# Softmax sums of batch 5 on GpSimd, and its key sums four gate slots later, in a fused attention and SwiGLU kernel

## The chip, the cores and the metric

The kernel runs on one core of one Trainium2 chip. The metric is the device time of one execution in microseconds (us), as a median of several runs. The profile shows one further execution; its span (231.4 us) runs from the first to the last instruction.

## The reference, cut to what matters

```python
# q, k, v: (8, 8, 576, 64); phi: (8, 8, 576, 32); batches, heads, positions, width
a = np.exp(phi - phi.max(2)); a = a / (a.sum(2) + 1e-9)
k_m = np.einsum('bhsm,bhsd->bhmd', a, k)      # 576 keys become 32
v_m = np.einsum('bhsm,bhsd->bhmd', a, v)
scores = q @ k_m.T / sqrt(64)
attn_out = softmax(scores) @ v_m
x = attn_out as (8 * 576, 512)
out = (silu(x @ w_gate) * (x @ w_val)) @ w_out     # 512 -> 1536 -> 512
```

What the change touches is the denominator of the first softmax, `np.sum(a, axis=2)`: for each of 8 heads and 32 memory slots, a sum of 576 exponentials. The kernel holds these exponentials of a batch as nine slices of 128 x 128 (`t_ephi`), with 64 of the positions of a head on the partitions, so the denominator is a sum over the nine slices and then over partitions.

## The kernel before, in words

The kernel works through eight batches. Each batch after the first two has a stage with two parts: a dense part, in which TensorE (PE) multiplies the hidden block of the batch before with the output weights and ScalarE and VectorE make the attention of this batch, and then 24 gate slots. A slot is one pair of gate matmuls, a SiLU on ScalarE (`gv_gate`), and the pair of value matmuls of the slot before with its multiplication on VectorE. Matmuls with `t_U` at line 515 are these gate and value products; those at line 727 are the output products (`p_os`, `p_oa`, `p_oc`).

The schedule is written out by hand: each engine runs its instructions in the order in which the program emits them. In the gate part, `spread` merges several streams into one order. A stream is a list of items with a first and a last slot number; item i of n gets the key first + (i + 0.5) * (last - first) / n, and the items are emitted in the order of their keys. The 24 slots have the keys 0.5, 1.5 and so on to 23.5.

Between the slots of batch b lies the preparation of batch b + 1. `kv_items` gives two items: the key and value sums with what goes with them (`run_sums`), and the transposition of the result by a DMA (`kv_T`, from `t_bkv` to `t_kT`). Their stream runs from `KV` = 6 to 10, so they have the keys 7.0 and 9.0: between slots 6 and 7, and between 8 and 9. Beside the sums stands a U round (`u_item(b, 2)`), which the slots from 16 on use, and two output units. At the keys 19 to 20 lies `u_three(b + 1)`, the first user of the transposed keys.

There are two forms of the sums:

- Without help: nine denominator products on TensorE (line 258, one for each slice of `t_ephi`) into a bank of their own, the reciprocal on VectorE, then 72 key and value products (line 230), scaling on VectorE, then the U round and the two units.
- With `phi_sum` (lines 212 to 219): GpSimd (POOL) adds the nine slices in float32 and writes the sum as two bf16 parts, `t_ehl`. Then `run_sums` does the 72 products first, the U round and the two units, and only then two denominator products from `t_ehl`, the reciprocal and the scaling.

Batches 4, 6 and 7 take the second form (`phi_sum(b + 1)` in the stages of batches 3, 5 and 6); batches 2, 3 and 5 take the first.

In the stage of batch 4, GpSimd has a further job. Each batch has 576 positions, of which 64 are left over by the tiling of the output products; those of four batches are collected and multiplied together. `quad_sums(0)` makes the sums for that, twelve additions and subtractions on GpSimd (`t_Q` and `t_x`, lines 664 and 560). It starts behind `wait_for(atts[4, 1])`, a small copy that holds GpSimd's queue until the normalized scores of batch 4 exist (`t_mark<-t_A`). In the gate part the quad's output units lie in slots 0 to 3 (twelve units) and from 12 to 18.5 (thirty units); the last units of batch 3 lie in slots 4 to 7. Between slots 7 and 12 there are gate slots alone. Later in the same stage GpSimd makes the sums of the hidden blocks of batch 4 (`t_S`, from line 603 on), and issues the loads of batch 7.

Of the kernel before, what the change touches and what calls it, by code (L numbers as in the profile page):

```python
# [14 lines left out]
def kernel(  # L15
# [59 lines left out]
    def bank(shape, dtype, name):  # L75
        tag = free.pop(0)
        t = ps.tile(shape, dtype, tag=tag, name=name)
        held[id(t)] = tag, t
        return t

    def done(*tiles):

        for t in tiles:
            free.append(held.pop(id(t))[0])
# [29 lines left out]
    def load_qT(b):  # L114

        qTs[b] = att.tile([128, NS, 128], BF16, tag="qT", name="t_qT")
        nc.sync.dma_start_transpose(out=qTs[b], in_=qs[b])
# [87 lines left out]
    def phi_sum(b):  # L205

        e = ephis[b].rearrange("p j i m -> p j (i m)")
        wait_for(atts[b - 1, 1][0:1, 0, 0:1])  # L210
        t = att.tile([128, 4, 128], FP32, tag="es", bufs=1, name="t_es")
        add = lambda o, x, y: nc.gpsimd.tensor_tensor(out=o, in0=x, in1=y, op=ALU.add)
        add(t, e[:, 0:4], e[:, 4:8])
        add(t[:, 0:2], t[:, 0:2], t[:, 2:4])
        add(t[:, 0], t[:, 0], t[:, 1])
        add(t[:, 0], t[:, 0], e[:, 8])
        hl = att.tile([128, 2, 128], BF16, tag="ehl", bufs=1, name="t_ehl")
        nc.gpsimd.tensor_copy(out=hl[:, 0], in_=t[:, 0])
        nc.gpsimd.tensor_tensor(out=hl[:, 1], in0=t[:, 0], in1=hl[:, 0], op=ALU.subtract)
        esums[b] = hl  # L220

    def kv_sum(b, p, parts):


        w0, w1 = parts[0], parts[-1] + 1
        n = (w1 - w0) * D
        for j in range(JK):
            for i in range(NP):
                for g in range(NG):
                    nc.tensor.matmul(  # L230
                        p[g][32 * i:32 * i + 32, 0:n],
                        lhsT=phi_of(b, g, j, i),
                        rhs=kvs[b][64 * g:64 * g + 64, w0:w1, i, j * D:(j + 1) * D],
                        start=(j == 0),
                        stop=(j == JK - 1),
                        tile_position=(64 * g, 32 * i),
                    )

    def kv_denominators(b, p):

        if b in masked:
            for g in range(NG):
                for j in range(JK):
                    nc.tensor.matmul(
                        p[:, g:g + 1],
                        lhsT=masked[b][:, j, g].rearrange("p i m -> p (i m)"),
                        rhs=ones1,
                        start=(j == 0),
                        stop=(j == JK - 1),
                    )  # L250
            return
        if b in esums:
            hl = esums.pop(b)
            terms = [hl[:, t] for t in range(2)]
        else:
            terms = [ephis[b][:, j].rearrange("p i m -> p (i m)") for j in range(JK)]
        for n, x in enumerate(terms):
            nc.tensor.matmul(p, lhsT=x, rhs=ones2, start=(n == 0), stop=(n == len(terms) - 1))

    def kv_reciprocal(b, p):  # L260
        r = att.tile([128, NG], FP32, tag="rS", name="t_rS")
        nc.vector.reciprocal(out=r, in_=p)
        rSs[b] = r
# [28 lines left out]
    def kv_items(b, beside=None):  # L292


        def run_sums():
            o = 2 * D
            behind = b in esums
            own = beside and not behind
            if own:
                d = bank([128, NG], FP32, "p_S")  # L300
                kv_denominators(b, d)
                kv_reciprocal(b, d)
                done(d)
            p = [bank([128, CH], FP32, f"p_kv{g}") for g in range(NG)]
            if not (own or behind):
                kv_denominators(b, p[0][:, o:o + NG])
            kv_sum(b, p, (0, 1))
            if behind:
                beside()
                kv_denominators(b, p[0][:, o:o + NG])  # L310
            if not own:
                kv_reciprocal(b, p[0][:, o:o + NG])
            kv_norm(b, p)
            if beside and not behind:
                beside()

        return [run_sums, lambda: kv_T(b)]
# [324 lines left out]
    def wait_for(x):  # L642

        t = att.tile([1, 1], BF16, tag="mark", bufs=1, name="t_mark")
        nc.gpsimd.tensor_copy(out=t, in_=x)
# [183 lines left out]
    def q_items(b, evac):  # L829
        return [lambda n=n: q_T(b, n, evac[n]) for n in range(3)]  # L830

    def u_item(b, c, evac="avav"):

        return lambda: u_round(b, (((0,), c, (0, 1)), ((1,), c, (0, 1))), evac)
# [13 lines left out]
    def run(items):  # L848
        for x in items:
            x()  # L850
# [10 lines left out]
    def exp_tables():  # L861
        nc.scalar.preload_act_table_set("natural_log_exp_and_others")
# [111 lines left out]
    def take(n):  # L974
        nonlocal backlog
        n = max(0, min(n, len(backlog)))
        part, backlog = backlog[:n], backlog[n:]
        return part

    KV = 6  # L980
# [15 lines left out]
    for b in range(2, B):  # L996
        last = b + 1 == B
        exp_tables()
        if b == 2:
            load_qT(3)  # L1000
            phi_exp(2)
            (zero, ops0), (one, ops1) = products(0, ("c11",)), products(1, ("p1", "c11"))
            kv, q2 = kv_items(2), q_items(2, "aaa")
            run(zero[:6])
            sums = {n: f for n, f in zip(((1, 1), (0, 2), (1, 2)), late)}
            late.clear()
            sums[0, 2]()
            weight_sums(0)
            weight_sums(1)
            run(zero[6:12] + one[:6] + kv[:1] + q2[:2])  # L1010
            weight_sums(2, (0, 1))
            run(zero[12:16] + zero[18:22] + kv[1:] + q2[2:] + zero[16:18] + zero[22:24])
            weight_sums(2, (2, 3))
            ops0["c11"]()
            ops1["p1"]()
            wait_for(Ts[2][0:1, 3, 0, 0:1])
            for part in ((0, 1), (3,), (2,)):
                for c in (1, 2):
                    sums[1, c](part)
            loads(4)  # L1020
            backlog = one[6:12] + zero[36:] + one[12:36]
            ops = ops1
        else:
            run(take(6))
        for g in range(NG):
            scores(b, g)
        if b > 2:
            ops["p1"]()
            u_values(b)
        else:  # L1030
            run(zero[24:36] + take(6))
        run(take(6))
        z_inv_v(b, 0)
        ops["c11"]()
        run(take(6))
        if not last:
            phi_exp(b + 1)
        z_inv_v(b, 1)
        if b > 2:
            norm(b, 0)  # L1040
            norm(b, 1)
        run(take(6))
        run_late()
        if b == 4:
            wait_for(atts[4, 1][0:1, 0, 0:1])
            quad_sums(0)
        nc.scalar.preload_act_table_set("silu_and_others")
        run(take(6))
        if b == 2:
            norm(2, 0)  # L1050
        run(take(6))
        if b == 2:
            norm(2, 1)
            u_three(2)
            run(one[36:])
        g = gv_slots(b)
        quad = []
        if b == 4:
            quad = products(b, (), 0)[0]
        if last:  # L1060
            rest, rest_ops = products(b, (), 1)
            backlog += rest[:12]
        beside = 0 if last else 2 if quad else min(4, len(backlog))
        outs = [lambda: run(take(1)) for _ in range(len(backlog) - beside)]
        streams = [(g, 0, 24), (quad[:12], 0, 3), (quad[12:], 12, 18.5)]
        streams += [(outs, 4, 7 if quad else 24)]
        if b == 2:
            streams += [([lambda: u_values(2)], 2.5, 3)]
        if last:
            streams += [([u_item(b, 2)], 5, 6)]  # L1070
        if not last:
            if b > 2:
                load_qT(b + 1)
            if b > 2 and b != 4:
                phi_sum(b + 1)
            streams += [
                (kv_items(b + 1, lambda: (u_item(b, 2, "aava")(), run(take(2)))), KV, KV + 4),
                ([lambda: (u_three(b + 1), run(take(2)))], 19, 20),
            ]
        spread(*streams)  # L1080
        flush_mul()
        units, ops = products(b, ("p1", "c11"))
        backlog += units
# [34 lines left out]
```

## Time and profile before

| | |
|---|---|
| time, median of three runs | 233.22 us (233.15 to 233.31) |
| span of the profiled run | 231.4 us |
| mean granted TensorE clock | 0.997 |
| gate part of batch 4 | 123.69 to 143.63 us |
| GpSimd's leftover sums in it | 123.33 to about 130.9 us |
| key sums of batch 5 | from 128.84 us |

In the profile's rows the first number is the start in us from the span's start, the second the duration; then engine, line, operation, output and inputs with their shape, and how many like instructions were merged. [...] the spacing of starts, and not the sum of durations, tells what TensorE's queue pays. A bracket at the end gives the idle time of the engine ahead of the row and what ended it. `PEld` is TensorE's weight load, `DVE` is VectorE, `ACT` ScalarE, `POOL` GpSimd and `SPq` the queue from which stores and transposing DMAs are issued.

### The profile page before, as it was taken

The page shows a single profiled execution, that of the slowest core. Times are in us where ns is not written, and L with a number is a line of the kernel's source. Part 1 is how long each engine was busy: PE and PEld are TensorE (multiplying, and loading weights), DVE is VectorE, ACT ScalarE, POOL GpSimd, SP SyncE. Part 2 cuts the span into 40 slices and gives each one's busy share as a digit, 9 for nine tenths or more (in the row PEclk, how much of TensorE's full clock was granted, in tenths as well). Part 3 has the DMA queues.
Part 4 walks back from the last instruction along what each step waited for, and adds up shares of the span by engine and source line. Part 5 has one row for each costly group of instructions (what it writes and reads, how often), then busy time and mean ns, then how long its engine had stood idle before and what let it go on. Part 6 is the DMA issues. An engine that isn't in the chain of part 4 may idle for free.

```text
span 231.4 us, 7210 instructions
## 1 busy us (share of the span) xinstructions
PE 221.6 (96%) x2825; PEld 169.8 (73%) x2825; DVE 185.1 (80%) x423; ACT 171.7 (74%) x365; POOL 140.8 (61%) x190
## 2 busy tenths in 40 slices
PE   6987799999999999999999999999999999999993
PEld 2544476778887777878788787887788778878882
DVE  4245789999966799989997668998999899977732
ACT  2777898988447989968896658978898789677310
POOL 8422427998199049765977689464845394039291
PEclk9999999999999999999999999999999999999998
DMA  6999999999996992999299946994014502202125
GB/s 214 210 211 206 199 207 207 221 245 268 205 225 175 256 256 49 223 204 184 71 223 191 226 134 115 252 236 89 28 65 114 104 0 95 91 10 84 31 85 160
DMA packets 36674, 36.84 MB, mean 159 GB/s; under 512 B 14624, under 2 KB 31008, under 8 KB 36640
## 3 DMA queue, kind: packets, MB, share of 16 engines
q0 software_dynamic: 16272, 22.42, 52.5%
q1 hardware_dynamic: 19600, 13.18, 22.9%
q10 hardware_dynamic: 768, 0.79, 1.1%
q8 instruction: 22, 0.36, 0.6%
q14 instruction: 12, 0.10, 0.1%
HBM read 42.47 MB, written 9.44 MB: 224 GB/s over the span
## 4 chain that ended last, share of the span: by engine, by line
PE 86%; DMA 9%; POOL 2%; ACT 1%; issue 0%; DVE 0%; POOLq 0%
PE p_g L515 21%; PE p_os L727 21%; PE p_v L515 20%; PE p_oc L727 10%; DMA W<-in_moe_w_val_dram 9%; PE p_oa L727 5%; PE p_u L472 5%; PE p_kv L230 2%; PE p_g L396 1%; POOL t_kv L99 1%; POOL t_kv L103 1%; PE p_q L383 0%; POOL t_q L108 0%; ACT t_qT L337 0%; POOL W L138 0%
## 5 line engine op out<-in xcount | busy, mean ns | idle before, releaser
L538 DVE TENSOR_TENSOR t_h<-t_sg,p_v 128x288 bf16<-128x288 bf16 x192 | 81.8, 451 | 14.1 <-PE p_v L515 7.0
L515 PEld LDWEIGHTS <-t_U 128*128 128x128 bf16 x768 | 73.9, 98 | 21.2 <-issue 3.5
L532 ACT ACTIVATE t_sg<-p_g 128x288 bf16<-128x288 f32 x192 | 73.3, 424 | 17.1 <-PE p_g L515 11.4
L515 PE MATMUL p_g<-t_A,t_U 128*128 128x288 bf16 x384 | 77.0, 286 | 0.0
L515 PE MATMUL p_v<-t_A,t_U 128*128 128x288 bf16 x384 | 77.0, 286 | 0.0
L727 PEld LDWEIGHTS <-t_S 128*128 128x128 bf16 x384 | 37.5, 98 | 4.5 <-issue 0.2
L603 POOL TENSOR_TENSOR t_S<-t_h 128x512 bf16<-128x512 bf16 x17 | 19.7, 1157 | 32.7 <-DVE t_h L538 31.2
L727 PEld LDWEIGHTS <-t_h 128*128 128x128 bf16 x288 | 27.1, 98 | 8.6 <-issue 5.0
L492 ACT CAST t_U<-p_u 128x512 bf16<-128x512 f32 x51 | 27.0, 605 | 6.6 <-PE p_u L472 6.6
L727 PE MATMUL p_os<-t_T,t_S 128*128 128x256 bf16 x192 | 23.7, 273 | 0.0
L560 POOL TENSOR_TENSOR t_S<-t_S,t_h 128x512 bf16<-128x512 bf16 x17 | 19.6, 1156 | 1.3
L560 POOL TENSOR_TENSOR t_S<-t_h 128x512 bf16<-128x512 bf16 x16 | 18.4, 1152 | 0.0
L560 POOL TENSOR_TENSOR t_S<-t_h,t_S 128x512 bf16<-128x512 bf16 x16 | 18.4, 1152 | 0.0
L472 PE MATMUL p_u<-W,t_kT 64*32 64x512 bf16 (+1 forms) x416 | 15.3, 363 | 1.2 <-DMA W<-in_moe_w_gate_dram 0.6
L496 DVE CAST t_U<-p_u 128x512 bf16<-128x512 f32 x21 | 13.6, 683 | 1.9 <-PE p_u L472 1.9
L727 PE MATMUL p_os<-t_T,t_h 128*128 128x256 bf16 x96 | 14.8, 273 | 0.0
L875 PE MATMUL p_warm<-bones 128*128 128x512 bf16 x44 | 12.5, 421 | 1.7 <-DVE bones L897 1.7
L452 DVE TENSOR_TENSOR t_A<-t_E,t_lz 128x576 bf16<-128x576 bf16 x16 | 11.4, 740 | 0.7 <-ACT t_lz L428 0.7
L727 PE MATMUL p_oc<-t_T,t_S 128*128 128x256 bf16 x96 | 11.9, 273 | 0.0
L727 PE MATMUL p_oa<-WO,t_h 128*128 128x256 bf16 x96 | 11.8, 273 | 0.0
L727 PE MATMUL p_oc<-WO,t_S 128*128 128x256 bf16 x96 | 11.8, 272 | 0.1
L727 PE MATMUL p_os<-WO,t_h 128*128 128x256 bf16 x96 | 11.8, 273 | 0.0
(107 smaller groups left out, 308.3 us busy)
## 6 DMA issues: line engine op xcount, KB each, us to landing
out_dram<-t_o SPq DMA_DIRECT2D x11, 512.0 KB, 3.0
t_kv<-in_k_dram POOLq DMA_DIRECT2D x8, 576.0 KB, 10.5
t_q<-in_q_dram POOLq DMA_DIRECT2D x8, 576.0 KB, 8.4
t_kv<-in_v_dram POOLq DMA_DIRECT2D x8, 576.0 KB, 14.7
t_phi<-in_phi_dram POOLq DMA_DIRECT2D x6, 576.0 KB, 8.1
out_dram<-t_o SPq DMA_DIRECT2D x10, 256.0 KB, 4.5
WO<-in_moe_w_out_dram POOLq DMA_DIRECT2D x3, 512.0 KB, 19.2
W<-in_moe_w_gate_dram POOLq DMA_DIRECT2D x2, 512.0 KB, 16.5
```

Of the source, the lines that this page charges most:

```text
L230: nc.tensor.matmul(p[g][32 * i:32 * i + 32, 0:n], lhsT=phi_of(b, g, j, i), rhs=kvs[b][64 * g:64 * g + 64, w0:w1, i, j * D:(j + 1) * D], st ...
L452: nc.vector.tensor_tensor(out=a, in0=es.pop((b, g)), in1=lzs.pop((b, g)), op=ALU.mult)
L472: nc.tensor.matmul(p[g][32 * i:32 * i + 32, o:o + n], lhsT=kTs[b][64 * g:64 * g + 64, 2, 32 * i:32 * i + 32], rhs=w_part(w, c, i, g, halve ...
L492: nc.scalar.copy(out=t, in_=p)
L496: nc.vector.tensor_copy(out=t, in_=p)
L515: nc.tensor.matmul(p[:, 0:HALF], lhsT=Us[b, c, g][:, o // 2, which, 128 * (o % 2):128 * (o % 2 + 1)], rhs=atts[b, g][:, r], start=(g == 0) ...
L532: nc.scalar.activation(out=sg, in_=gate[:, 0:HALF], func=AF.Silu)
L538: nc.vector.tensor_tensor(out=dst, in0=sg, in1=val[:, 0:HALF], op=ALU.mult)
L560: eng.tensor_tensor(out=out, in0=x, in1=y, op=ALU.subtract)
L603: eng.tensor_tensor(out=t[:, 0], in0=A21, in1=A22, op=ALU.add)
L727: nc.tensor.matmul(mine[home][:, u], lhsT=lhs(c, m, u), rhs=rhs(c, m), start=fresh and u == 0, stop=(k == 5), skip_group_check=u == 1 or n ...
L875: nc.tensor.matmul(p[:, 0:128 * a], lhsT=bones, rhs=x.to_broadcast([128, a, 128]) if a > 1 else bones, start=True, stop=True,)
```

## The change

Batch 5 takes the second form as well: in the stage of batch 4, GpSimd also sums the nine exponentials of batch 5, in its queue behind the leftover sums. This replaces nine denominator products on TensorE by two. So that the sum has time to be made, the stream of batch 5's key sums is put four slots later: `run_sums` gets the key 11.0 (between slots 10 and 11) and `kv_T` 13.0. Nothing else moves.

```diff
@@ -1071,10 +1071,11 @@
         if not last:
             if b > 2:
                 load_qT(b + 1)
-            if b > 2 and b != 4:
+            if b > 2:
                 phi_sum(b + 1)
+            first = KV + 4 if b == 4 else KV
             streams += [
-                (kv_items(b + 1, lambda: (u_item(b, 2, "aava")(), run(take(2)))), KV, KV + 4),
+                (kv_items(b + 1, lambda: (u_item(b, 2, "aava")(), run(take(2)))), first, first + 4),
                 ([lambda: (u_three(b + 1), run(take(2)))], 19, 20),
             ]
         spread(*streams)
```

## The prediction

> **What bounds the kernel now.** I read the shares of the engines first, then the chain of work that ended last, then TensorE (PE) and GpSimd (POOL) in order of time around batch 4, and last the same places one batch later, where the kernel already works as the change wants it.
>
> ```profile
> PE 221.6 (96%) x2825; PEld 169.8 (73%) x2825; DVE 185.1 (80%) x423; ACT 171.7 (74%) x365; POOL 140.8 (61%) x190
> ```
>
> ```profile
> PE 86%; DMA 9%; POOL 2%; ACT 1%; issue 0%; DVE 0%; POOLq 0%
> ```
>
> The first line is busy time by engine, the second the chain's shares. TensorE is 96% busy and carries 86% of the chain; its DMA part is the load of weights before 27 us. From there to the end the chain is TensorE's own queue nearly without a break. So a microsecond that TensorE gains or loses in the middle moves the end by about a microsecond. GpSimd is 61% busy and has room on average, but the question is whether it has room at one place.
>
> TensorE, around the key sums of batch 5 in batch 4's gate slots (start, duration, operation):
>
> ```profile
> 128.84 0.37 PE L258 MATMUL p_S<-ones,t_ephi 128*128 128x2 bf16 x9
> 129.14 0.80 PE L230 MATMUL p_kv<-t_kv,t_ephi 64*32 64x128 bf16 x72
> 129.73 0.66 PE L472 MATMUL p_u<-W,t_kT 64*32 64x512 bf16 x16
> 130.32 0.61 PE L727 MATMUL p_os<-t_T,t_h 128*128 128x256 bf16 x4
> 130.76 0.41 PE L515 MATMUL p_g<-t_A,t_U 128*128 128x288 bf16 x2
> ...
> 132.86 0.41 PE L515 MATMUL p_g<-t_A,t_U 128*128 128x288 bf16 x2
> ```
>
> Nine denominator products, 72 key products, the U round of chunk 2, two output units, then gate slot 7 at 130.76; the row at 132.86 is the gate of slot 11. Differences of starts give the cost: 1.92 us for the block (128.84 to 130.76), 2.10 us for slots 7 to 10.
>
> GpSimd at the same time (the bracket is idle time ahead of the row):
>
> ```profile
> 128.98 1.92 POOL L560 TENSOR_TENSOR t_Q<-t_x,t_Q 128x256 bf16<-128x256 bf16 x3
> 133.13 1.15 POOL L603 TENSOR_TENSOR t_S<-t_h 128x512 bf16<-128x512 bf16 x1 [2.24 <-DVE t_h L538]
> ```
>
> The leftover sums `quad_sums(0)` are twelve operations from 123.33; the row at 128.98 is the last three, so GpSimd comes free at about 130.86 (rows overlap by some 0.03: 127.10 + 1.91 is 129.01, and the next starts at 128.98). It then idles 2.24 us until the first chunk of batch 4's hidden activations is whole.
>
> What the sum of nine costs on GpSimd, from batch 5, where it exists:
>
> ```profile
> 152.15 0.18 POOL L645 COPY t_mark<-t_A 1x1 bf16<-1x1 bf16 x1 [2.78 <-DVE t_A L452]
> 152.29 1.14 POOL L212 TENSOR_TENSOR t_es<-t_ephi 128x512 f32<-128x512 bf16 x1
> 153.52 1.26 POOL L212 TENSOR_TENSOR t_es<-t_es 128x256 f32<-128x256 f32 x2
> 154.85 0.43 POOL L212 TENSOR_TENSOR t_es<-t_es,t_ephi 128x128 f32<-128x128 f32 x1
> 155.35 0.29 POOL L218 CAST t_ehl<-t_es 128x128 bf16<-128x128 f32 x1
> 155.72 0.43 POOL L219 TENSOR_TENSOR t_ehl<-t_es,t_ehl 128x128 bf16<-128x128 f32 x1
> ```
>
> From the marker's start to the end of the subtraction: 155.72 + 0.43 - 152.15 = 4.00 us. The same seven operations take 4.00 us in batch 3 and 3.98 us in batch 6.
>
> And TensorE there:
>
> ```profile
> 155.12 0.41 PE L515 MATMUL p_v<-t_A,t_U 128*128 128x288 bf16 x2
> 155.46 0.80 PE L230 MATMUL p_kv<-t_kv,t_ephi 64*32 64x128 bf16 x72
> 156.04 0.66 PE L472 MATMUL p_u<-W,t_kT 64*32 64x512 bf16 x16
> 156.63 0.61 PE L727 MATMUL p_os<-t_T,t_h 128*128 128x256 bf16 x4
> 157.08 0.19 PE L258 MATMUL p_kv<-ones,t_ehl 128*128 128x2 bf16 x2
> 157.13 0.40 PE L515 MATMUL p_g<-t_A,t_U 128*128 128x288 bf16 x2
> ```
>
> The two denominator products start at 157.08, 0.93 us after the sum was ready at 156.15, so they wait for nothing. The margin is under a microsecond although GpSimd started its sum with no other work ahead of it after the marker.
>
> [...]
>
> **The change part by part.**
>
> 1. Products. Nine products become two, and move behind the U round. Block with nine: 1.92 us. Block with two: the value row at 155.12 hands over 0.245 us later (half of the 0.49 us of a bare slot), at 155.365, and the next gate starts at 157.13: 1.765 us. Gain 0.155 us, all on TensorE.
>
> 2. Place. The key 6 + 1 = 7.0 becomes 10 + 1 = 11.0, so the block falls behind slot 10 instead of slot 6. Four bare slots now come first. With the block just done, ScalarE had three copies of U and one of the output behind it, and slots 7 to 10 took 2.10 us; bare slots that are not behind such a block take 0.49 us each (154.87 less 154.38 on TensorE one batch later), so 1.96 us. Gain 0.14 us. After the block the quad's output units start again (from slot 12), where ScalarE and VectorE have room.
>
> 3. When TensorE asks for the sum: 128.84 + 1.96 (slots 7 to 10) + 0.10 (the step to the key products, as at 155.365 to 155.46) + 0.58 (key products) + 0.59 (U round) + 0.45 (two units) = 132.52 us.
>
> 4. When GpSimd has it. In its queue the sum stands behind all twelve leftover sums, which start only when the second normalized block exists (marker at 123.19 us). So 130.86 + 4.00 = 134.86 us. I take the hand-over to TensorE as 0.13 us, as from the end of the normalization on VectorE (123.06) to GpSimd's marker (123.19)[...]. With 0.10 for a weight load (LDWEIGHTS 98 ns) the last product starts at 135.09 and the gate of slot 11 at about 135.16.
>
> 5. **The new wait.** TensorE stands 135.09 - 132.52 = 2.57 us. Behind the waiting product in its queue are the value of slot 10 and everything later, on which ScalarE and VectorE depend. Nothing passes it. The gate of slot 11 moves from 132.86 to 135.16: 2.30 us net, with gains 1 and 2 already inside (2.57 - 0.155 - 0.14 is 2.28; the rest is rounding and the exposed weight load).
>
> 6. What is costed at nothing. The sum takes GpSimd's idle 2.24 us and pushes chunk 0's sums from 133.13 to 134.86; they then end near 139.5 us. Chunk 1's sums wait for VectorE until 138.90 today, which itself moves to about 141.2, so GpSimd has caught up by then. The loads of batch 7 go out behind these, about 2.3 us later, like TensorE; their data are used two batches on, over 30 us later. VectorE's reciprocal and four scalings (0.16 + 0.99 us) now come after the wait and delay its next multiplication by about 1 us, but slots 12 on contain output units and there are five banks free. The transposed keys: issued 133.99 today, landing 5.0 us later, used at 140.64. After: denominators plus 1.55 us (157.08 to the issue at 158.59, 1.51) gives about 136.6; with landings of 2.3 to 5.0 us, 138.9 to 141.6, against a use at about 142.9. Hidden, by 1.3 us at worst.
>
> Sum: 233.22 + 2.30 = 235.5 us.
>
> **The rivals.** (a) The wait is hidden and only gains 1 and 2 stay: 233.22 - 0.30 = 232.9 us. For it: batches 3, 5 and 6 run this form without a wait, and four slots were added. Against: four bare slots are 1.96 us, while GpSimd's leftover sums push the sum 7.5 us past the marker that elsewhere starts it at once; it would have to end 2.3 us earlier than any measured duration allows. (b) The wait comes and TensorE's clock falls too. [...] Against: TensorE is busy on both sides. (c) A part is recovered: ScalarE and VectorE enter slot 11 with empty queues, and slots 7 to 10 might already run slower than 0.49. Taking back about 0.8 us: 234.7. Against: after 133 us TensorE starts pairs at full rate with hardly a gap to give back.
>
> **How the numbers follow.** Forecast (the full wait) 0.77, with 235.1 to 235.9 for the hand-over's ends and a few tenths of recovery; (a) 0.08; (b) 0.06; (c) 0.09. The range 234.6 to 236.2 holds the forecast and most of (c), and leaves (a) and (b) out. Faster only under (a): 0.07, with 0.02 for no change; slower 0.91.
>
> **What would show it.** Right: a TensorE gap of about 2.6 us ahead of the two denominator products near 135 us, put down to GpSimd's subtraction; t_ehl written near 134.9 us; the gate of slot 11 near 135.2; later stages as long as before. Wrong: t_ehl before 132.5 us, the gap shorter than 2 us, a clock under 1.00 between 133 and 139 us, or TensorE waiting for the transposed keys at the U round of batch 5.

## The result, and the profile after

| | before | after |
|---|---|---|
| time, median of 6 executions each | 233.25 us (233.15 to 233.43) | 236.84 us (235.44 to 237.04) |
| ratio, 95% interval | | 1.0136 (1.0107 to 1.0166) |
| span of the profiled execution | 231.4 us | 235.1 us |

The change makes the kernel about 1.4% slower; 235.5 us was forecast, with a range up to 236.2. The executions of the changed kernel fall into two groups with nothing between: two at 235.44 and 235.51 us with a mean granted TensorE clock of 0.999 and 1.000, four from 236.77 to 237.04 us with a clock of 0.990 to 0.993. The profile is one of the second group.

TensorE in the changed kernel, in order of time, from the U round ahead of the two denominator products on:

```profile
131.49 0.66 PE L472 MATMUL p_u<-W,t_kT 64*32 64x512 bf16 x16
132.09 0.61 PE L727 MATMUL p_os<-t_T,t_h 128*128 128x256 bf16 x4
134.36 0.18 PE L258 MATMUL p_kv<-ones,t_ehl 128*128 128x2 bf16 x1 [1.66 <-POOL t_ehl L218]
134.86 0.18 PE L258 MATMUL p_kv<-ones,t_ehl 128*128 128x2 bf16 x1 [0.33 <-POOL t_ehl L219]
134.90 0.41 PE L515 MATMUL p_g<-t_A,t_U 128*128 128x288 bf16 x2
135.14 0.41 PE L515 MATMUL p_v<-t_A,t_U 128*128 128x288 bf16 x2
135.39 0.53 PE L727 MATMUL p_os<-t_T,t_Q 128*128 128x256 bf16 x2
135.71 0.69 PE L515 MATMUL p_g<-t_A,t_U 128*128 128x288 bf16 x2
136.19 0.69 PE L515 MATMUL p_v<-t_A,t_U 128*128 128x288 bf16 x2
```

Two things stand here. First the wait: the two output units from 132.09 (four matmuls) are through TensorE's queue at about 132.53 (0.44 us, as their spacing in the kernel before), and the products come at 134.36 and 134.86, each put down to the GpSimd write that it needs. In the 2.3 us between, TensorE issues one product of two columns. The gate of slot 11 starts at 134.90; before it was 132.86. Second, from 135.5 us on the same pairs are slower: a gate pair takes 0.48 us from start to start (135.71 to 136.19) where it took 0.24 (134.90 to 135.14).

GpSimd in the same stretch:

```profile
128.96 1.91 POOL L560 TENSOR_TENSOR t_Q<-t_x,t_Q 128x256 bf16<-128x256 bf16 x3
130.83 0.18 POOL L645 COPY t_mark<-t_A 1x1 bf16<-1x1 bf16 x1
130.97 1.15 POOL L212 TENSOR_TENSOR t_es<-t_ephi 128x512 f32<-128x512 bf16 x1
...
134.38 0.43 POOL L219 TENSOR_TENSOR t_ehl<-t_es,t_ehl 128x128 bf16<-128x128 f32 x1
134.76 1.15 POOL L603 TENSOR_TENSOR t_S<-t_h 128x512 bf16<-128x512 bf16 x1
```

It is never idle: the last leftover sums, the marker, the sum of nine, written at 134.38 + 0.43 = 134.81 us, and at once the first sums of the hidden block.

The slower pairs are the clock. The stretches of one microsecond, with the granted clock (PEclk) as the third number from the end, then the DMA share and GB/s; TensorE's busy time is the second number:

```profile
134.00:135.00 1.00, 0.32 (x3) 0.24 (x4) 0.00 (x0) 0.06 (x1) 0.91 (x3) 1.00 0.59 136
135.00:136.00 1.00, 1.00 (x9) 0.73 (x7) 0.89 (x4) 0.41 (x1) 0.92 (x2) 0.74 1.01 383
136.00:137.00 1.00, 1.00 (x6) 0.67 (x5) 0.65 (x4) 0.41 (x1) 1.00 (x1) 0.50 0.42 148
137.00:138.00 1.00, 1.00 (x7) 0.66 (x6) 0.44 (x1) 0.23 (x1) 1.00 (x2) 0.50 0.48 98
138.00:139.00 1.00, 1.00 (x6) 0.67 (x5) 0.00 (x0) 0.55 (x2) 1.00 (x2) 0.55 0.08 12
139.00:140.00 1.00, 1.00 (x11) 0.84 (x10) 0.46 (x1) 0.45 (x2) 0.72 (x2) 1.00 0.05 5
```

At half clock, 0.74 in one microsecond means 0.52 us of it and 0.55 means 0.90 us, so the clock is down from about 135.48 to 138.90, for 3.4 us. That begins 0.6 us after TensorE is back at work. Note how little of it the profile's page gives away: in its row of 40 slices the clock shows one 7 among nines, and TensorE is counted as busy all through.

The chain of work that ended last, in shares by engine, now has GpSimd with 7% where it had 2%:

```profile
PE 78%; DMA 8%; POOL 7%; DVE 3%; issue 1%; ACT 1%; DVEq 0%; POOLq 0%
```

### The profile page after: what moved, and what is told of

The parts are those of the page before. It is cut to its first block, busy times and chain, and to the rows that moved or that the text cites. A ratio compares the mean times of both kernels' runs of the same rounds, so it can differ in the third digit from the quotient of the medians.

```text
span 235.1 us, 7204 instructions
## 1 busy us (share of the span) xinstructions
PE 223.6 (95%) x2818; PEld 170.5 (73%) x2818; DVE 185.2 (79%) x423; ACT 172.1 (73%) x365; POOL 144.1 (61%) x197
## 4 chain that ended last, share of the span: by engine, by line
PE 78%; DMA 8%; POOL 7%; DVE 3%; issue 1%; ACT 1%; DVEq 0%; POOLq 0%
PE p_g L515 20%; PE p_v L515 19%; PE p_os L727 18%; PE p_oc L727 9%; DMA W<-in_moe_w_val_dram 8%; PE p_u L472 5%; PE p_oa L727 4%; POOL t_Q L560 2%; PE p_kv L230 2%; POOL t_es L212 1%; POOL t_x L560 1%; POOL t_Q L664 1%; POOL t_kv L99 1%; POOL t_kv L103 1%; DVE t_z L435 1%
## 5 line engine op out<-in xcount | busy, mean ns | idle before, releaser
L875 PE MATMUL p_warm<-bones 128*128 128x512 bf16 x44 | 13.0, 434 | 1.7 <-DVE bones L897 1.7
```

The lines of the kernel that those rows point to most:

```text
L875: nc.tensor.matmul(p[:, 0:128 * a], lhsT=bones, rhs=x.to_broadcast([128, a, 128]) if a > 1 else bones, start=True, stop=True,)
```

## The experiments

Theory A: the change costs a wait of TensorE for GpSimd's sum, about 2 us in every execution, and the idle stretch lets the clock fall in some executions, another 1.5 us. Rivals: B, the further loss is a delay of its own and not the clock's; C, the later place of the key sums costs the time, not the sum; D, the clock falls for the load of the chip and not for idleness. Ratios below are against the kernel before on the same chip in the same series. There were three such series, each on another chip: again, first4, place4 and warm; kv5, kv6, first0 and early4; behind3, behind0, first5 and first6.

**again.** No edit.

> The changed kernel once more, for the share of executions in which TensorE's clock falls behind the wait. Theory A (the wait for GpSimd's sum costs 2.2 us always, and the idle stretch of about 2.3 us it makes lets the clock fall for 3.4 us in some executions, another 1.4 to 1.7 us): two groups, near 235.5 and near 236.9 us, nothing between, and a granted clock of 1.00 in the first and 0.99 in the second. Rival B (the further 1.4 us is a delay of its own, of a DMA or of GpSimd's later sums): the times do not go with the clock.

236.72 us, ratio 1.0116 (1.0089 to 1.0144). Executions: 235.09 and 235.40 us at a clock of 0.999; 236.68, 236.77, 236.90 and 237.08 us at 0.992 or 0.993. With the six above, 8 of 12 have the fall; their mean is 236.89 us, that of the other four 235.36, so the fall costs 1.5 us. The wait alone costs about 2: 2.2 us in the first series and 1.7 in this one, where the kernel before took 233.57 us. Time and clock go together in all twelve, against B. The profile of this run is one without a fall, and its wait is the same (1.67 and 0.33 us).

**first4.** GpSimd's order turned round.

```diff
         if b == 4:
-            wait_for(atts[4, 1][0:1, 0, 0:1])
+            phi_sum(5)
             quad_sums(0)
...
-            if b > 2:
+            if b > 2 and b != 4:
                 phi_sum(b + 1)
```

> GpSimd makes the sum of nine ahead of the leftover sums instead of behind them; the place (four slots later) and the two products stay. Theory A: the sum is ready near 127.3 us, TensorE asks for it at 132.5, no wait and no fall of the clock; the leftover sums end near 134.7 instead of 130.8 and are asked for from 133 us on one by one, so nothing else waits: 232.9 us. Rival C (what costs the time is the later place, for the keys' transposition or the U round, and not the sum): stays near 235 us or more.

233.26 us against 233.57: 0.9979 (0.9969 to 0.9990). Place and products are those of the change, only the order on GpSimd differs, and the whole loss is gone. C falls. The gain of 0.30 us that the prediction put into products and place lies inside this interval (0.1 to 0.3%), but the times don't settle it: the kernel before spread from 233.04 to 234.73 us here, and between the fastest executions of the two are 0.07 us. TensorE's rows show a gain that is there and then mostly lost:

```profile
132.49 0.19 PE L258 MATMUL p_kv<-ones,t_ehl 128*128 128x2 bf16 x2
132.56 0.40 PE L515 MATMUL p_g<-t_A,t_U 128*128 128x288 bf16 x2
133.05 0.41 PE L515 MATMUL p_v<-t_A,t_U 128*128 128x288 bf16 x2
```

The gate of slot 11 comes 0.30 us earlier than in the kernel before (132.86). But from gate to value are 0.49 us instead of 0.24: a hole of 0.25 us. ScalarE's copies of the U round run from 131.92, three in 1.56 us, so the second ends near 133.0, when the value starts. By the order in which banks come free, this value takes the second bank that these copies empty. That reading fits the times; the bank itself is not in the trace.

**place4.** The four slots alone.

```diff
-            if b > 2:
+            if b > 2 and b != 4:
                 phi_sum(b + 1)
```

> The four later slots alone: nine denominator products, no sum on GpSimd. Theory A: only the slower bare slots behind the block are gained, 0.14 us: 233.1 us, clock 1.00. Rival C (the place costs the time): 235 us or more.

233.31 us, ratio 0.9993 (0.9983 to 1.0002): no loss from the place, against C, and a gain of 0.14 us is neither shown nor excluded.

**first0.** The edit of GpSimd's order from first4, the key sums where they were.

> The sum ahead of the leftover sums, the key sums at their old place (key 7.0), two products. Theory A: the sum is ready near 127.2 us and asked for near 130.6: no wait; 0.15 us gained by seven products fewer: 233.1 us, where 233.2 to 233.6 was measured for the kernel before.

233.42 us, ratio 1.0003 (0.9995 to 1.0011). The seven products fewer bring nothing that can be measured. Two holes of 0.24 us of the kind in first4 (130.83 to 131.31, and 131.80 to 132.29) take back what the products gave. TensorE doesn't come to these slots earlier than in the kernel before (the gate of slot 7 at 130.83 us, there 130.76, with ScalarE's copies from 130.19 and 130.20). What differs is the order of the banks. The program hands out a bank in the order in which banks were given back. With nine products the two banks of the key sums are given back ahead of the U round; with two, behind it, so the next slots take the banks of the U round and of the output, which ScalarE empties:

```profile
130.19 1.56 ACT L492 CAST t_U<-p_u 128x512 bf16<-128x512 f32 x3 [1.00 <-PE p_u L472]
131.63 0.62 ACT L337 COPY t_o<-p_os 128x512 f32<-128x512 f32 x1
```

By equal shares the second copy ends near 131.23, and the output's at 132.25, each less than 0.1 us ahead of the end of a hole. The times fit this reading closely; no run with another order of banks tests it.

**warm.** TensorE kept at work through the wait.

```diff
-    (kv_items(b + 1, lambda: (u_item(b, 2, "aava")(), run(take(2)))), first, first + 4),
+    (kv_items(b + 1, lambda: (u_item(b, 2, "aava")(), run(take(2)),
+                              b == 4 and warm(36))), first, first + 4),
```

> The changed kernel with nine matmuls of 512 columns on constants, into a bank that nothing reads, between the two output units and the two denominator products: TensorE works for about 1.9 us of its wait. Theory A: the wait for the sum ends at the same time, so the time is 235.5 us in every execution, and the clock never falls (1.00): it is the idle stretch that lets it fall. Rival B, and a rival D (the clock falls for the load of the chip, not for idleness): the group near 236.9 us stays, or the matmuls come on top.

235.37 us, all six between 235.15 and 235.46, clock 0.997 to 1.000; ratio 1.0074 (1.0059 to 1.0089). TensorE in this kernel:

```profile
132.73 2.10 PE L875 MATMUL p_warm<-bones 128*128 128x512 bf16 x9
134.67 0.17 PE L258 MATMUL p_kv<-ones,t_ehl 128*128 128x2 bf16 x1
135.04 0.18 PE L258 MATMUL p_kv<-ones,t_ehl 128*128 128x2 bf16 x1 [0.20 <-POOL t_ehl L219]
135.08 0.40 PE L515 MATMUL p_g<-t_A,t_U 128*128 128x288 bf16 x2
```

Matmuls that nobody reads make the kernel 1.4 us faster than the changed one in the median. The wait ends where it did (the second product comes 2.82 us behind the start of the two units, in the changed kernel 2.77), so they cost nothing, and in none of six executions does the clock fall, against 4 of 6 in the run named again, on the same chip. B and D fall: idleness is the cause, and 235.4 us is the time with the wait alone.

**behind3, kv5, kv6, behind0.** The wait made longer and shorter by the place of the key sums; the sum stays behind the leftover sums.

```diff
-            first = KV + 4 if b == 4 else KV
+            first = KV + 3 if b == 4 else KV      # behind3; 5 in kv5, 6 in kv6, 0 in behind0
```

> The changed kernel with the key sums three slots later instead of four (key 10.0): the sum stays behind the leftover sums, TensorE asks for it 0.49 us earlier. Theory A: a wait of about 2.8 us; 235.6 to 236.0 us without a fall of the clock, 237.1 to 237.5 with one, and the fall in more executions than 8 of 12 (2.3 us idle), since none of 5 had it at 1.8 us. Rival D (the fall has nothing to do with the length of the idle stretch): about two thirds again.

> The changed kernel with the key sums five slots later instead of four (key 12.0). TensorE then works one more bare slot (0.49 us) before it asks for the sum. Theory A: the wait shrinks from about 2.3 to about 1.8 us; without a fall of the clock 234.9 us. If the clock falls for the length of the idle stretch, the share of executions near 236.4 us is below the 8 in 12 seen with 2.3 us. Rival D (the clock falls for the load of the chip): the share is as before.

> The key sums six slots later (key 13.0): two slots and five one-matmul units of the quad more before TensorE asks, 1.5 us. Theory A: a wait of about 0.75 us is left, and no fall of the clock: 233.7 us, all executions within 0.5 us of each other. Rival C: later is worse, since the transposed keys come later: 235 us or more.

> The sum behind the leftover sums and the key sums at their old place (key 7.0): TensorE asks for it near 130.6 us and has it near 135, a wait of about 4.2 us. Theory A: 237.4 us for the wait alone, and the clock falls in every execution, so 238.8 to 239.3 us. Rival: the time that the later place takes away is lost elsewhere, and this is no slower than 236.9 us.

| run | slots later | idle, us | time, us | ratio (95%) | clock fell in |
|---|---|---|---|---|---|
| kv6 | 6 | 0.8 | 233.80 | 1.0019 (1.0010 to 1.0027) | 0 of 12 |
| kv5 | 5 | 1.9 | 234.75 | 1.0067 (1.0053 to 1.0081) | 0 of 5 |
| change | 4 | 2.3 | 236.84 | 1.0136 (1.0107 to 1.0166) | 8 of 12 |
| behind3 | 3 | 2.8 | 236.02 | 1.0120 (1.0099 to 1.0142) | 2 of 6 |
| behind0 | 0 | 4.3 | 238.84 | 1.0227 (1.0214 to 1.0240) | 5 of 5 |

The idle time is from the end of the units in the queue (their start and 0.44 us) to the second product, with the first product inside it. "Fell" is a mean clock of 0.990 to 0.993; all others are 0.996 or more. The row of the change has the time and ratio of the first series, and the falls of that and of again. In the longest, TensorE's rows around the wait:

```profile
130.39 0.61 PE L727 MATMUL p_os<-t_T,t_h 128*128 128x256 bf16 x4
134.63 0.18 PE L258 MATMUL p_kv<-ones,t_ehl 128*128 128x2 bf16 x1 [3.63 <-POOL t_ehl L218]
135.14 0.19 PE L258 MATMUL p_kv<-ones,t_ehl 128*128 128x2 bf16 x1 [0.33 <-POOL t_ehl L219]
135.19 0.64 PE L515 MATMUL p_g<-t_A,t_U 128*128 128x288 bf16 x2
```

The wait follows the place slot by slot, and at 4.3 us the clock fell in all five executions. 238.84 is 0.4 us less than 233.48 (before in that series), 4.3 and 1.5 together; about 0.2 of it is that here the clock falls 0.4 us before TensorE is back at work, and the rest is not accounted for.

But the share is not in order: 2.8 us gave fewer falls than 2.3, and my expectation of a larger share was not met. With 2 of 6 against 8 of 12 that can be chance, and the two were measured on different chips. The traces show that the length alone doesn't settle it. By the brackets in its rows TensorE idles for 0.50 us of the wait in kv6, 1.55 in kv5, 1.99 in the change, 2.00 in again, 2.48 in behind3 and 3.96 in behind0. In the profiles of the change and of behind0 the clock falls; in that of again it is 1.00 from 123.2 to 145 us, and in that of behind3 from 125 to 142. So there was a fall with 1.99 us of idle time and none with 2.00 and 2.48. What else decides it was not shown.

**early4.** The sum ahead of everything on GpSimd, without its marker.

```diff
         if b == 4:
+            phi_sum(5)            # its own wait_for left out for batch 5
             wait_for(atts[4, 1][0:1, 0, 0:1])
             quad_sums(0)
...
-            if b > 2:
+            if b > 2 and b != 4:
                 phi_sum(b + 1)
```

> The sum ahead of the leftover sums and without its own marker copy, so that it fills GpSimd's idle stretch before the normalization (from 120.4, or from the exponentials at 121.4 us); key sums four slots later. Theory A: no wait, the leftover sums end near 133 us instead of 134.6: 232.9 to 233.2 us. A rival: GpSimd's float additions beside VectorE's reductions and normalization lengthen these, and the first gate at 123.7 us waits for them: 0.3 to 1 us more.

234.11 us, ratio 1.0035 (1.0022 to 1.0048): the rival was right. VectorE's normalization, first in the kernel before, then here, with what GpSimd does beside it (line numbers are one higher in this kernel):

```profile
121.68 1.38 DVE L452 TENSOR_TENSOR t_A<-t_E,t_lz 128x576 bf16<-128x576 bf16 x2
121.91 2.77 DVE L453 TENSOR_TENSOR t_A<-t_E,t_lz 128x576 bf16<-128x576 bf16 x2
122.94 2.05 POOL L213 TENSOR_TENSOR t_es<-t_es 128x256 f32<-128x256 f32 x2
```

TensorE's first gate:

```profile
124.73 0.28 PE L516 MATMUL p_g<-t_A,t_U 128*128 128x288 bf16 x1 [0.51 <-DVE t_A L453]
```

The two normalizing multiplications took 1.38 us and take 2.77 beside GpSimd's float additions, and the first gate waits 0.51 us. GpSimd's own pair of additions takes 2.05 us here and 1.26 elsewhere, so they take longer beside the normalization too, where step 4 of the prediction reckoned with one duration for the whole sum, 4.00 us. The marker copy, which looks like idle time of GpSimd, keeps the two apart.

**first5, first6.** As first4, with the key sums five and six slots later.

```diff
-            first = KV + 4 if b == 4 else KV
+            first = KV + 5 if b == 4 else KV      # 6 in first6
```

> The sum ahead of the leftover sums, as in first4, with the key sums five slots later (key 12.0). In first4 a hole of 0.24 us stands behind the two products: the value of slot 10 takes a bank of the U round that ScalarE empties only at its second copy. At key 12.0 two or three units of the quad, which need no new bank, come right behind the products. Theory A: the hole closes, 0.2 us less than first4: about 0.3% below the kernel before. Rival: the hole comes one slot later, and the time is that of first4.

> As first5 at key 13.0, in the midst of the quad's units. Theory A: as first5, without the hole; the leftover sums that the next units need (the last are written near 134.6 us) are asked for a little later, so no wait there either: 0.2 to 0.3% below the kernel before. Rival: the transposed keys, now issued near 136 us, come too late for the U round of batch 5 near 140.5 us: up to 1 us more.

first5: 233.08 us against 233.48, ratio 0.9976 (0.9968 to 0.9985), the fastest of all, 0.2% faster than the kernel before. Units come right behind the products and the hole shrinks to 0.04 us (133.85 to 134.14 from gate to value); against first4 (0.9979) the gain is inside the intervals. first6: 233.34 us, 0.9996 (0.9988 to 1.0004). There two holes follow the products (0.29 us ahead of 134.60 and 0.17 ahead of 136.04), where none was expected, and the keys come too late, as its rival had it, by a smaller amount:

```profile
141.08 0.84 PE L472 MATMUL p_u<-W,t_kT 64*32 64x512 bf16 x24 [0.23 <-DMA t_kT<-t_bkv]
```

## Why the prediction was right and wrong

- **The wait: right, in mechanism and nearly in size.** GpSimd was forecast to have the sum at 134.86 us and had it at 134.81; TensorE to ask at 132.52 and asked at about 132.53; the gate of slot 11 to move by 2.30 us and it moved by 2.04. Most of the 0.26 us too much is the hand-over and weight load of step 4: 0.23 us were added from the sum to the last product, and 0.05 were measured (134.81 to 134.86). Executions without the fall have 235.36 us where 235.5 was forecast.
- **The clock, put at nothing in the sum: the step that failed.** The sum, 233.22 and 2.30 us, has no term for it, and rival (b), which has it, got 0.06. The fall came in 8 of 12 executions and cost 1.5 us, which puts the median at 236.84. That the clock outlasts the forecast stretch of 2.57 us was the author's estimate, and no trace had shown it. That TensorE "is busy on both sides" did not help: of the 3.41 us ahead of the fall at 135.48 us, it has work for 0.46 us ahead of the wait and 0.62 behind it. The clock then stood at 0.50 for 3.41 us.
- **A sign in the trace of before was missed.** Between 118.40 and 152.18 us the clock of that trace is 1.00. But its mean is 0.997, and it is down at 0.50 from 230.12 us to the end, 2.5 us after TensorE's last product (227.60). So a fall behind 2.5 us of rest stood in that very trace. With a forecast stretch of 2.57 us, a range that reaches beyond 236.2 us would have been right.
- **Gains 1 and 2 (0.30 us): there, but not kept for certain.** At the gate of slot 11 they are there (first4: 132.56 against 132.86). The hole behind it takes most of them back. In the times, first0 holds gain 1 alone and shows none of it, place4 holds gain 2 alone and fits both 0.14 us and nothing, and first4 with both fits 0.30. Step 6 said that five banks are free behind the block; the holes of 0.24 us in first0 and first4 fit slots that wait for banks which ScalarE is still emptying. In the changed kernel the wait for GpSimd hides this.
- **Step 6 otherwise: right.** The transposed keys were issued at 136.34 us (136.6 forecast), and nothing waited for them in this kernel; GpSimd was idle again from 139.7 us, before chunk 1 was whole.
- **Rival (a)** needed a sum ready by 132.5 us. first4 does just that with another order, and lands within 0.4 us of the 232.9 given for it.

## What to carry to other kernels

Before work is moved to a less busy engine, put its finish time (what stands ahead in that queue, plus its own duration) beside the time at which the bounding engine asks for it; a share of 61% busy says nothing about that moment. When the answer is an idle stretch of TensorE like the one of 2.3 us here (a fall in 8 of 12 executions, 1.5 us each; none in 5 at 1.9 us), price a second loss for the clock next to the stretch itself, and look for it in stretches of a microsecond, since the shares on the profile's page hide it. Then take more than one execution: a single profile shows a fall or none, for the same wait (1.66 and 0.33 us with one here, 1.67 and 0.33 without one in again). The cure here was order: the urgent job ahead of the patient one on the same queue.

## What the runs showed of the hardware

The traces show TensorE's clock at 0.50 in two places. One is the wait: in the changed kernel it falls at 135.48 us and returns at 138.89, 3.41 us later; in behind0 it falls at about 134.76, still within the wait, and returns at about 138.18. The other is the end: in the kernel before it falls at 230.12 us, 2.5 us after the end of TensorE's last row, and in the changed kernel at 234.47, 3.15 us after it (231.32). The first two lines are from the changed kernel, ahead of the fall and from it on, the next two from the kernel before at its end (TensorE's busy time, by the durations of its rows, is the second number, the clock the third from the end):

```profile
132.07:135.48 3.41, 1.42 (x19) 0.93 (x12) 1.06 (x3) 2.13 (x5) 3.03 (x7) 1.00 1.11 150
135.48:138.89 3.41, 3.41 (x17) 2.27 (x16) 1.61 (x6) 1.46 (x4) 3.33 (x4) 0.50 0.44 135
...
226.70:230.12 3.42, 0.90 (x8) 0.49 (x6) 0.88 (x3) 0.00 (x0) 0.00 (x0) 1.00 0.67 180
230.12:231.40 1.28, 0.00 (x0) 0.00 (x0) 0.00 (x0) 0.00 (x0) 0.00 (x0) 0.50 0.00 0
```

TensorE was not wholly idle ahead of these falls: it has 1.42 us of work in the 3.41 us ahead of the one and 0.90 us in the 3.42 us ahead of the other. And an idle stretch does not always bring a fall: again has the wait of the changed kernel (1.67 and 0.33 us), and the clock stays at 1.00.

In early4 VectorE's normalization took 2.77 us with GpSimd's float additions at the same time, and 1.38 us without them in the kernel before.
